# Top-32 attention and two expert layers on one core: score products of a pair of tiles back to back and first, one score copy per pair

## The chip, the cores and the metric

One core of one Trainium2 chip. The time is device microseconds for the whole program, from launch to the last output; three runs of the kernel before stand below, and their median is the time to compare with. All stretches are given in microseconds from the start of the profiled span.

## What is computed

Three layers in sequence. Attention: 4 batches, 8 heads, 576 tokens, head width 64; in every row only the 32 largest scores stay. Then a two-matrix layer with a squared ReLU on 2304 tokens, then a layer in which each token goes to one of eight experts.

```python
scores = scale * np.matmul(q, k.transpose(0, 1, 3, 2))
kth = np.partition(scores, -top_k, axis=-1)[..., -top_k:-top_k + 1]
scores = np.where(scores >= kth, scores, -1000000000.0)
attn = np.exp(scores - np.max(scores, axis=-1, keepdims=True))
attn = attn / (np.sum(attn, axis=-1, keepdims=True) + 1e-09)
x = np.matmul(attn, v)
...
r = np.maximum(x @ w_in, 0.0)
x = (r * r) @ w_out
...
e_idx = np.argmax(xc @ w_gate, axis=1)
y[mask] = gate_w[mask, None] * (np.maximum(xc[mask] @ w1[e], 0.0) @ w2[e])
```

## The kernel before

**Tiles and pairs.** The attention works on 144 tiles of 128 query rows by 576 keys, two at a time: 72 pairs, one pair per turn of the main loop (line 667). fp32 operands are split into a high and a low fp16 part, so a score tile is 2 products for each of three groups of 192 keys, 6 in all, and 12 for a tile that joins the 64 left-over rows of two heads.

**A pair's way through the engines.** PE makes the scores of both tiles in one PSUM tile `pS` (`qk`, line 326). There is one such buffer. ACT copies each tile's scores to SBUF as `s` (`evac_s`, line 334), two copies per pair. DVE builds from `pS` and `s` the arrays of larger and smaller halves `tr` (`tree`, line 351), and only when it has read `pS` may the next pair's scores be written. Then DVE finds the 32 largest values by four rounds of MAX8 (line 370) and three of MATCH_REPLACE8 (line 373). ACT derives the exponent's bias `nm` from the first round (line 378) and takes the exponentials (line 392); DVE makes the mask `mk` (line 397); POOL applies it (line 405); ACT rounds to fp16 and sums (line 420), POOL forms the low part (line 425), a DMA transposes, and three pairs later PE multiplies with V (`av`, line 448) and ACT scales the result (line 466). ACT also keeps three of each tile's 32 values for a later test: `keep_bounds`, line 401, once per pair.

**The tree of the next pair stands at the end of a pair's turn on DVE.** `tree(a + 2)` is put behind `top32(a)` and the two masks of the pair come behind it, so DVE needs the next pair's second score copy as soon as the current pair's fourth round is done.

**The first expert-like layer runs between the pairs.** From the tenth pair on, PE also does the products of the two-matrix layer for tokens that are finished: `mm1` (line 525, into `ph`), on ACT three passes (lines 533, 535, 537), on POOL one (line 546), and `mm2` (line 558, into `px`). A turn of the loop issues about 4.4 half units of it, in two parts; between them stand the scores of the next pair's second tile:

```python
        if nxt:
            qk(a + 2)
            evac_s(a + 2)
        conv(conv_act, j, 0, 2)
        step_units(HALVES / 2)
        if nxt:
            qk(b + 2)
            evac_s(b + 2)
        step_units(HALVES / 2)
```

What is left of that layer when the last pair is done runs after the attention; then come the routing and the experts.

**What sets the order.** The code's order is only the start: a scheduler with a model of the engines arranges the instructions of every engine when the program is built, and each engine then executes its own list strictly in order. The wait of one instruction holds everything behind it on that engine.

Of the kernel before, what the change touches and what calls it, by code (L numbers as in the profile page):

```python
# [9 lines left out]
F32 = mybir.dt.float32  # L10
# [5 lines left out]
AF = mybir.ActivationFunctionType  # L16
# [5 lines left out]
B, H, S, D = 4, 8, 576, 64  # L22
# [16 lines left out]
SB = 3  # L39
# [60 lines left out]
def attention_two_moes(ctx, tc, qm, qc, kd, vd, w_in, w_out, w_g, w1, w2, cst, out):  # L100
    nc = tc.nc
# [7 lines left out]
    apool = att_scope.enter_context(tc.tile_pool(name="att", bufs=1, side="right"))  # L109
# [18 lines left out]
    bounds = const.tile([128, B * H * S // 128, 3], F32, name="bounds")  # L128
# [177 lines left out]
    st = [dict() for _ in range(NTILE)]  # L306

    def kv(kind, vi, hd):
        return vq[kind, visits[vi]["b"], visits[vi]["pr"], hd]

    def qk(i):
        vi, tl = T[i]
        if i % 2 == 0:
            st[i]["ps2"] = st[i + 1]["ps2"] = side[0].tile([128, 2, 3, 256], F32, name="pS")
        ps = st[i]["ps"] = st[i]["ps2"][:, i % 2, :, :192]
        if tl[0] == "m":
            c0 = tl[1] * 128 if visits[vi]["half"] else tl[1] * 256 + tl[2] * 128
            jobs = [(vq[vi, "qm"][:, :, c0:c0 + 128], kv("k", vi, tl[1]))]
        else:
            q = vq[vi, "qc"]  # L320
            jobs = [(q[:, :, 0:128], kv("k", vi, 0)), (q[:, :, 64:192], kv("k", vi, 1))]
        for c in range(3):
            n = 0
            for q, kh in jobs:
                for part in range(2):
                    nc.tensor.matmul(ps[:, c], lhsT=q[:, part], rhs=kh[:, c * 192:(c + 1) * 192],  # L326
                                     start=(n == 0), stop=(n == 2 * len(jobs) - 1))
                    n += 1

    def evac_s(i):  # L330
        if i % 2 == 0:
            st[i]["s2"] = st[i + 1]["s2"] = apool.tile([128, 2, S], F32, name="s", bufs=SB)
        s = st[i]["s2"][:, i % 2]
        nc.scalar.activation(s.rearrange("p (a b) -> p a b", a=3), st[i]["ps"], AF.Copy,  # L334
                             scale=2.0 ** (-2 * QK_EXP))
        st[i]["s"] = s

    def pair_tiles(a):
        m = apool.tile([128, 2, 32], F32, name="m8", bufs=3)
        nm = apool.tile([128, 2], F32, name="nm", bufs=3)  # L340
        l = apool.tile([128, 2, 2], F32, name="l", bufs=6)
        for k in range(2):
            st[a + k].update(m=m[:, k], nm=nm[:, k:k + 1], l=l[:, :, k])
        st[a]["pair"] = (m, nm, l)

    def tree(a):
        R2 = apool.tile([128, 2, S], F32, name="tr")
# [50 lines left out]
        st[i]["mk"] = t  # L398

    def keep_bounds(a):  # L400
        nc.scalar.activation(bounds[:, a:a + 2], st[a]["pair"][0][:, :, 15::8], AF.Copy)

    def apply_mask(i):
        e = st[i]["e"]
# [223 lines left out]
    def fetch(j):  # L628
        for pc in by_rj.get(j, []):
            if "raw" not in pc:  # L630
                load_piece(pc)
# [11 lines left out]
    def conv(step, j, lo, hi):  # L643
        for it in conv_at.get(j, [])[lo:hi]:
            step(*it)
# [6 lines left out]
    conv(load_w64, -1, 0, 4)  # L652
    nc.sync.dma_start(wgs, w_g)
    qk(0)
    evac_s(0)
    qk(1)
    conv(conv_act, -1, 0, 2)
    conv(conv_dve, -1, 0, 2)
    conv(conv_split, -1, 0, 2)
    conv(conv_act, -1, 2, 4)  # L660
    conv(conv_dve, -1, 2, 4)
    evac_s(1)
    fetch(-1)
    conv(load_w64, 0, 0, 2)
    run_all(low_pool)

    for j in range(NJ + AV_LAG + 1):
        a, b = 2 * j, 2 * j + 1
        live = a < NTILE
        nxt = a + 2 < NTILE  # L670
# [6 lines left out]
        conv(conv_split, j - 1, 2, 4)  # L677
        conv(load_w64, j, 2, 4)
        if nxt:
            qk(a + 2)  # L680
            evac_s(a + 2)
        conv(conv_act, j, 0, 2)
        step_units(HALVES / 2)
        if nxt:
            qk(b + 2)
            evac_s(b + 2)
        step_units(HALVES / 2)
        conv(conv_dve, j, 0, 2)
        if live:
# [123 lines left out]
    pair = side[0].tile([128, 2, 512], F32, name="pS")  # L813
# [592 lines left out]
```

## Time and profile before

| | |
|---|---|
| median of three runs | 1046.55 us (1044.35, 1046.55, 1052.29) |
| the profiled execution, its own time | 1045.87 us |
| its span on the core | 1044.0 us |
| busy: DVE, PE, ACT, POOL | 845.9, 792.5, 772.9, 764.2 us (81, 76, 74, 73% of the span) |
| mean granted TensorE clock | 0.926 |

The program has three stretches that matter here. Until about 193 us the weights are converted beside the first twelve pairs. From 193 to 767 us the other sixty pairs run, about 9.6 us each, with the two-matrix layer between them. From 767 us the rest of that layer, the routing and the experts follow. The shares of the whole span mix these stretches, so every reading below is of one stretch. In the rows, "idle before" is the time in which an engine stood still ahead of an instruction, with what ended it; "PE" rows are products, and PEclk is the granted clock as a share of 2.4 GHz.

### The profile page before, as it was taken

To read this page: it belongs to the slowest core of one execution; us is meant where nothing else is said; L and a number is where in the kernel's file an instruction comes from. 1 tells how busy PE (TensorE), PEld (TensorE's weight loads), DVE (VectorE), ACT (ScalarE), POOL (GpSimd) and SP (SyncE) were. 2 spreads that over 40 slices of the span, in tenths; PEclk is the share of its full clock that TensorE was granted. 3 is DMA by queue.
4 is the path that set the end of the run, shared out by engine and by line. 5 is a ranking of instruction groups with operands and counts; after the bars stand their busy time and mean duration, and the time that the engine had idled before them with its cause. 6 is when DMAs were issued, how large, how long until landed. Compare 5 with 4: busy or idle time off the path is not lost. (4 is left out here: it accounts for less than half of the span.)

```text
span 1044.0 us, 25879 instructions
## 1 busy us (share of the span) xinstructions
PE 792.5 (76%) x9036; PEld 603.1 (58%) x9036; DVE 845.9 (81%) x2279; ACT 772.9 (74%) x2237; POOL 764.2 (73%) x783
## 2 busy tenths in 40 slices
PE   0213238989799879979879997979998876888863
PEld 0113137767577667667557775757776654565632
DVE  3999999989999999998997878899965927543641
ACT  6777777999889888887787887879987643443720
POOL 4675777898879888887788877788984686462860
PEclk9999999999889979989869998969999897998986
DMA  8765454567575474565575466454547616671600
GB/s 278 192 164 160 112 135 80 112 129 144 122 142 121 98 135 103 100 138 95 123 122 101 106 113 132 103 122 80 107 88 241 220 52 232 245 240 57 220 17 15
DMA packets 257024, 138.16 MB, mean 132 GB/s; under 512 B 215348, under 2 KB 238260, under 8 KB 256848
## 3 DMA queue, kind: packets, MB, share of 16 engines
q1 hardware_dynamic: 253568, 132.16, 54.0%
q0 software_dynamic: 3280, 3.80, 1.1%
q8 instruction: 93, 1.52, 0.6%
q14 instruction: 83, 0.68, 0.2%
HBM read 76.92 MB, written 7.37 MB: 81 GB/s over the span
## 5 line engine op out<-in xcount | busy, mean ns | idle before, releaser
L370 DVE MAX8 m<-tr 128x8 f32<-128x288 f32 (+1 forms) x576 | 276.8, 518 | 0.0
L405 POOL TENSOR_TENSOR e<-e,mk 128x576 f32<-128x576 f32 x144 | 196.1, 1374 | 25.7 <-DVE mk L397 25.7
L425 POOL TENSOR_TENSOR phl<-e,phl 128x576 f16<-128x576 f32 x144 | 187.3, 1309 | 14.7 <-ACT phl L420 13.0
L558 PE MATMUL px<-woh,gh 128*128 128x512 f16 x576 | 190.5, 381 | 10.0 <-POOL gh L546 6.5
L373 DVE MATCH_REPLACE8 tr<-m,tr 128x288 f32<-128x288 f32 x432 | 187.2, 439 | 0.0
L448 PE MATMUL misc<-vh,pt 128*128 128x64 f16 (+1 forms) x2400 | 124.2, 203 | 66.0 <-ACT xn L466 34.3
L525 PEld LDWEIGHTS <-wih 128*128 128x128 f16 x2048 | 145.0, 101 | 46.9 <-issue 13.3
L546 POOL TENSOR_TENSOR gh<-g,gh 128x128 f16<-128x128 f32 (+1 forms) x256 | 124.6, 492 | 64.8 <-ACT gh L537 47.0
L525 PE MATMUL ph<-xb,wih 128*128 128x128 f16 (+1 forms) x1792 | 159.9, 232 | 12.2 <-DMA xb<-xhl 10.0
L448 PEld LDWEIGHTS <-pt 128*128 128x128 f16 (+1 forms) x2400 | 104.9, 103 | 86.6 <-issue 57.2
L351 DVE SCALAR_TENSOR_TENSOR tr<-pS,s 128x576 f32<-128x576 f32 x144 | 102.2, 751 | 53.6 <-ACT s L334 51.3
L558 PEld LDWEIGHTS <-gh 128*128 128x128 f16 x864 | 77.5, 100 | 70.3 <-POOL gh L546 14.6
L326 PE MATMUL pS<-kh,ql 128*128 128x192 f16 x576 | 76.4, 279 | 48.5 <-DMA kh<-lp 18.2
L392 ACT ACTIVATE e<-s,nm 128x576 f32<-128x576 f32 x144 | 111.1, 773 | 1.4 <-POOL phl L425 0.8
L558 PE MATMUL px<-wol,gh 128*128 128x512 f16 x288 | 109.4, 380 | 0.0
L334 ACT ACTIVATE s<-pS 128x576 f32<-128x576 f32 x144 | 92.5, 642 | 18.3 <-PE pS L326 18.0
L420 ACT ACTIVATE phl<-e 128x577 f16<-128x577 f32 x144 | 98.2, 682 | 4.3 <-POOL e L405 3.8
L525 PE MATMUL ph<-xb,wil 128*128 128x128 f16 (+1 forms) x896 | 97.2, 231 | 0.0
L533 ACT ACTIVATE r<-ph 128x128 f32<-128x128 f32 (+1 forms) x256 | 72.0, 289 | 30.3 <-PE ph L525 28.3
L326 PEld LDWEIGHTS <-ql 128*128 128x128 f16 x576 | 56.9, 111 | 63.8 <-issue 43.0
L535 ACT ACTIVATE g<-r 128x128 f32<-128x128 f32 (+1 forms) x256 | 83.3, 327 | 8.7 <-POOL gh L546 5.1
L397 DVE TENSOR_SCALAR mk<-s,m 128x576 f16<-128x576 f32 x144 | 85.0, 631 | 0.0
(229 smaller groups left out, 1644.1 us busy)
## 6 DMA issues: line engine op xcount, KB each, us to landing
wraw<-in_w SPq DMA_DIRECT2D x64, 512.0 KB
wol<-in_w_in SPq DMA_DIRECT2D x16, 512.0 KB
raw<-in_qm SPq DMA_DIRECT2D x48, 128.0 KB
w<-in_w_out SPq DMA_DIRECT2D x10, 512.0 KB
raw<-in_vd SPq DMA_DIRECT2D x32, 160.0 KB
raw<-in_kd SPq DMA_DIRECT2D x16, 288.0 KB
out<-x SPq DMA_DIRECT2D x16, 256.0 KB
wol<-in_w_out SPq DMA_DIRECT2D x6, 512.0 KB
```

Source lines behind the costliest of these rows:

```text
L326: nc.tensor.matmul(ps[:, c], lhsT=q[:, part], rhs=kh[:, c * 192:(c + 1) * 192], start=(n == 0), stop=(n == 2 * len(jobs) - 1))
L351: last = nc.vector.scalar_tensor_tensor(out=R2[:, :, n * 288:n * 288 + 288].rearrange("p k (c x) -> p k c x", c=3), in0=near, scalar=2.0 * ...
L370: return both(lambda k: nc.vector.max(m[k][:, 8 * r:8 * r + 8], x[k][:, :n]))
L373: both(lambda k: nc.vector.match_replace(out=dst[k][:, :n], in_to_replace=m[k][:, 8 * r:8 * r + 8], in_values=src[k][:, :n], imm_value=NEG))
L392: nc.scalar.activation(e[:, :S], st[i]["s"], AF.Exp, scale=0.125, bias=st[i]["nm"])
L405: nc.gpsimd.tensor_mul(e[:, :S], e[:, :S], st[i]["mk"])
L420: nc.scalar.activation(h[:, 0, :S + 1], st[i]["e"], AF.Copy, accum_out=st[i]["l"][:, 0:1])
L425: nc.gpsimd.tensor_sub(h[:, 1, :S], st[i]["e"][:, :S], h[:, 0, :S])
L448: nc.tensor.matmul(ps[:, a, :], lhsT=pt[:rows, 5 * low + c, :], rhs=vh[:rows, c, part * D:(part + 1) * D], start=(n == 0), stop=(n == len( ...
L525: nc.tensor.matmul(ph, lhsT=wt[:, d, u["f"] * 128:(u["f"] + 1) * 128], rhs=x[:, :, c0 + d, :], start=(n == 0), stop=(n == 11))
L546: g_last[0] = nc.gpsimd.tensor_sub(u["gh"][:, 1], u["g"], u["gh"][:, 0]).ins
L558: nc.tensor.matmul(px, lhsT=gh[:, part, t * 128:(t + 1) * 128], rhs=w[:, f, :], start=(f == 0 and n == 0), stop=(f == 15 and n == 2))
```

## The change

Four edits. In the loop one call, `scores(a + 2)`, takes the place of the two separate steps: it issues the products of both tiles and one copy, under `tc.high_priority()`, which makes the scheduler take them ahead of other ready work. `evac_s` copies both tiles with one ACT instruction. The tile `m8` holds three pairs, and `keep_bounds` copies for three pairs at once. Before the loop, the first pair's copy stands behind the first weight conversions. In the changed kernel the lines behind these functions have numbers 9 or 10 higher, and behind the loop 5 higher.

```diff
-    def evac_s(i):
-        if i % 2 == 0:
-            st[i]["s2"] = st[i + 1]["s2"] = apool.tile([128, 2, S], F32, name="s", bufs=SB)
-        s = st[i]["s2"][:, i % 2]
-        nc.scalar.activation(s.rearrange("p (a b) -> p a b", a=3), st[i]["ps"], AF.Copy,
+    def evac_s(a):
+        s2 = apool.tile([128, 2, S], F32, name="s", bufs=SB)
+        nc.scalar.activation(s2.rearrange("p k (c x) -> p k c x", c=3), st[a]["ps2"][:, :, :, :192], AF.Copy,
                              scale=2.0 ** (-2 * QK_EXP))
-        st[i]["s"] = s
+        for k in range(2):
+            st[a + k].update(s2=s2, s=s2[:, k])
+
+    def scores(a):
+        with tc.high_priority():
+            qk(a)
+            qk(a + 1)
+            evac_s(a)
+
+    m6 = [None]
 
     def pair_tiles(a):
-        m = apool.tile([128, 2, 32], F32, name="m8", bufs=3)
+        if a % 6 == 0:
+            m6[:] = [m6[-1], apool.tile([128, 6, 32], F32, name="m8", bufs=3)]
+        m = m6[-1][:, a % 6:a % 6 + 2]
...
-        st[a]["pair"] = (m, nm, l)
+        st[a].update(pair=(m, nm, l), six=m6[-1])
...
     def keep_bounds(a):
-        nc.scalar.activation(bounds[:, a:a + 2], st[a]["pair"][0][:, :, 15::8], AF.Copy)
+        if a % 6 == 4:
+            nc.scalar.activation(bounds[:, a - 4:a + 2], st[a]["six"][:, :, 15::8], AF.Copy)
...
     qk(0)
-    evac_s(0)
     qk(1)
...
-    evac_s(1)
+    evac_s(0)
...
         if nxt:
-            qk(a + 2)
-            evac_s(a + 2)
+            scores(a + 2)
         conv(conv_act, j, 0, 2)
         step_units(HALVES / 2)
-        if nxt:
-            qk(b + 2)
-            evac_s(b + 2)
         step_units(HALVES / 2)
```

PE of the kernel before, the 46th pair (scores in `pS_7885`): here the six products of the first tile end, and products of probabilities with V follow.

```order
L326 LDWEIGHTS ql_7722
L326 MATMUL pS_7885<-kh_6476,ql_7722 128x192
L448 LDWEIGHTS pt_7680
L448 MATMUL misc_8024<-vh_7720,pt_7680 128x64
L448 LDWEIGHTS pt_7680
L448 MATMUL misc_8024<-vh_7720,pt_7680 128x64
```

And this is where the second tile of that pair begins, behind the products of the two-matrix layer's second half (`px`).

```order
L558 LDWEIGHTS gh_8708
L558 MATMUL px_7785<-woh_89,gh_8708 128x512
L558 LDWEIGHTS gh_8708
L558 MATMUL px_7785<-wol_87,gh_8708 128x512
L326 LDWEIGHTS ql_7722
L326 MATMUL pS_7885<-kh_6477,ql_7722 128x192
```

Between the two places stand 54 other products. PE of the changed kernel, the same pair (`pS_7782`), at the step from the first tile (keys `kh_6391`) to the second (`kh_6392`):

```order
L326 LDWEIGHTS ql_7622
L326 MATMUL pS_7782<-kh_6391,ql_7622 128x192
L326 LDWEIGHTS ql_7622
L326 MATMUL pS_7782<-kh_6391,ql_7622 128x192
L326 LDWEIGHTS ql_7622
L326 MATMUL pS_7782<-kh_6392,ql_7622 128x192
L326 LDWEIGHTS ql_7622
L326 MATMUL pS_7782<-kh_6392,ql_7622 128x192
```

Nothing stands between the two tiles any more. ACT of the kernel before, the 43rd pair: the second row behind its first copy is the first row here, and its second copy (`s_7492<-pS_7485`) is the last.

```order
L533 ACTIVATE r_7964<-ph_7919 128x256
L466 ACTIVATE xn_7306<-misc_7549,l_7016 128x64
L466 ACTIVATE xn_7308<-misc_7549,l_7016 128x64
L535 ACTIVATE g_7966<-r_7964 128x256
L537 ACTIVATE gh_7968<-r_7964 128x256
L533 ACTIVATE r_8084<-ph_7951 128x256
L392 ACTIVATE e2_94<-s_7328,nm_7508 128x576
L242 ACTIVATE vh_7720<-raw_7537 128x5x64
L535 ACTIVATE g_8086<-r_8084 128x256
L537 ACTIVATE gh_8088<-r_8084 128x256
L401 ACTIVATE bounds_85<-m8_7507 128x6
L334 ACTIVATE s_7492<-pS_7485 128x576
```

ACT of the changed kernel, the same pair: the bias of the pair before it (`nm_7410`) and the one copy of both tiles (`s_7402<-pS_7389`).

```order
L387 ACTIVATE nm_7410<-m8_7124 128x2
L430 ACTIVATE phl2_100,l_7297<-e2_94 128x577
L221 ACTIVATE raw_7338<-raw_7338 128x256
L332 ACTIVATE s_7402<-pS_7389 128x1152
L430 ACTIVATE phl0_98,l_7297<-e0_92 128x577
L401 ACTIVATE e1_93<-s_7241,nm_7410 128x576
L476 ACTIVATE xn_7213<-misc_7450,l_6925 128x64
L476 ACTIVATE xn_7215<-misc_7450,l_6925 128x64
L543 ACTIVATE r_7835<-ph_7797 128x256
L401 ACTIVATE e2_94<-s_7241,nm_7410 128x576
L543 ACTIVATE r_7860<-ph_7822 128x256
L411 ACTIVATE bounds_85<-m8_7124 128x18
```

The copy has moved from the end of the pair's ACT work to its beginning. Over the 14th to the 72nd pair the copy that completes a pair's scores stands 11 instructions behind the bias of the pair before it in the middle case, and 13 ahead of its own pair's bias; in the changed kernel 3 behind and 21 ahead. On DVE the order of the instructions of these pairs is the same in both kernels.

## Rows read from the trace of the kernel before

**Rows 1.** Busy time by stretch: start:end, length, engines, PEclk, DMA share, GB/s

```profile
core 0: us, PE busy (x) PEld busy (x) DVE busy (x) ACT busy (x) POOL busy (x), PEclk, DMA share, GB/s
193.00:767.00 574.00, 511.75 (x6053) 394.25 (x6050) 526.47 (x1527) 494.63 (x1573) 472.58 (x523) 0.92 0.59 115
536.00:637.00 101.00, 96.69 (x1075) 73.07 (x1076) 78.48 (x232) 85.09 (x257) 78.27 (x86) 0.98 0.58 110
767.00:858.00 91.00, 80.12 (x868) 59.34 (x866) 52.44 (x168) 58.67 (x190) 63.07 (x83) 0.96 0.52 164
858.00:1044.00 186.00, 127.89 (x1354) 93.54 (x1353) 90.88 (x168) 75.56 (x120) 97.77 (x63) 0.84 0.42 144
```

**Rows 2.** Waits from 193 to 767 us: total us, times, longest

```profile
DVE tr L351 <- ACT s L334: 43.6, 27, 4.3
...
ACT s L334 <- PE pS L326: 14.7, 10, 3.6
...
PE pS L326 <- ACT s L334: 9.4, 11, 1.4
...
PE pS L326 <- DVE tr L351: 3.5, 3, 1.9
```

**Rows 3.** Timeline around the 46th pair: start us, us, instruction, idle before

```profile
501.44 1.04 PE L525 MATMUL ph<-xb,wih 128*128 128x256 f16 x8
502.31 0.66 PE L326 MATMUL pS<-kh,ql 128*128 128x192 f16 x6
502.81 1.35 PE L448 MATMUL misc<-vh,pt 128*128 128x64 f16 x30
504.09 0.61 PE L525 MATMUL ph<-xb,wil 128*128 128x256 f16 x4
...
508.20 0.59 PE L558 MATMUL px<-woh,gh 128*128 128x512 f16 x2
508.63 0.38 PE L558 MATMUL px<-wol,gh 128*128 128x512 f16 x1
508.85 0.66 PE L326 MATMUL pS<-kh,ql 128*128 128x192 f16 x6
...
510.23 1.42 DVE L351 SCALAR_TENSOR_TENSOR tr<-pS,s 128x576 f32<-128x576 f32 x2 [1.56 <-ACT s L334]
```

**Rows 4.** Timeline around the 43rd pair

```profile
475.51 0.66 PE L326 MATMUL pS<-kh,qm 128*128 128x192 f16 x6
...
479.20 0.22 ACT L401 ACTIVATE bounds<-m 128x6 f32<-128x6 f32 x1
479.31 0.66 ACT L334 ACTIVATE s<-pS 128x576 f32<-128x576 f32 x1
...
480.00 1.42 DVE L351 SCALAR_TENSOR_TENSOR tr<-pS,s 128x576 f32<-128x576 f32 x2 [3.40 <-ACT s L334]
```

**Rows 5.** Groups by line, 193 to 767 us: busy us, mean ns, idle before

```profile
L351 DVE SCALAR_TENSOR_TENSOR tr<-pS,s 128x576 f32<-128x576 f32 x118 | 83.8, 751 | 45.7 <-ACT s L334 43.6
...
L334 ACT ACTIVATE s<-pS 128x576 f32<-128x576 f32 x118 | 75.9, 644 | 14.8 <-PE pS L326 14.7
...
L401 ACT ACTIVATE bounds<-m 128x6 f32<-128x6 f32 x59 | 13.0, 220 | 0.4
```

**Rows 6.** Groups by line, whole span: an ACT copy of 1024 elements

```profile
L870 ACT ACTIVATE w10h<-wraw 128x1024 f16<-128x1024 f32 x12 | 12.2, 1048 | 6.2 <-PEq L1131 4.1 <-DMA wraw<-in_w 2.0
```

**Rows 7.** Busy time, 767 to 858 us, of line 525 alone, then of line 558 alone

```profile
767.00:858.00 91.00, 37.03 (x516) 33.60 (x516) 0.96 0.52 164
...
767.00:858.00 91.00, 38.18 (x140) 12.59 (x138) 0.96 0.52 164
```

**Rows 8.** Busy time by 4 us, columns as in rows 1

```profile
444.00:448.00 4.00, 0.69 (x6) 0.69 (x7) 4.00 (x15) 4.00 (x12) 3.27 (x3) 1.00 0.39 107
448.00:452.00 4.00, 2.09 (x23) 1.85 (x22) 4.00 (x8) 1.68 (x6) 3.15 (x3) 0.54 1.07 221
452.00:456.00 4.00, 4.00 (x38) 3.07 (x37) 4.00 (x17) 3.86 (x10) 4.00 (x4) 0.61 0.54 106
```

## Prediction, made before the changed kernel ran

> **What bounds the kernel now.** I read the busy times by stretch first, then the waits of the pairs' stretch, then the timeline at two pairs where DVE waited, and last the stretch behind the attention.
>
> In the stretch of the last sixty pairs, 193 to 767 us, DVE is busy for 526.5 of 574.0 us, PE for 511.8, ACT for 494.6 and POOL for 472.6 [rows 1]. All four are loaded, but DVE most, and it has almost one reason to stand still: 43.6 of its 47.5 idle us are 27 waits of the tree for a score copy [rows 2]. That is what the change goes for. From one tree to the next there are 59 steps, so a pair takes 574.0 / 59 = 9.73 us now, and 526.5 / 59 = 8.92 us if DVE never waited.
>
> Why is the copy late? Two pairs show two causes. At the 46th, PE makes the first tile's scores at 502.31 us and the second's only at 508.85 us: 54 other products stand between them in its list. The tree starts at 510.23 us, after 1.56 us of idling [rows 3]. At the 43rd, PE is done at 475.51 + 0.66 = 476.17 us, but ACT copies the second tile only at 479.31 us, behind the other instructions that its list has ahead of it, the last of them the copy of the bounds; DVE idles 3.40 us [rows 4]. So the second tile is late once on PE and once on ACT, and in both cases by its place in a list, not by its own length.
>
> PE is the second bound, locally: between 536 and 637 us it is busy 96.7 of 101 us at a clock of 0.98, while DVE is busy for 78.5 [rows 1]. Behind the attention, from 767 to 858 us, PE is busy 80.1 of 91 us with the rest of the two-matrix layer; the 186 us from there to the end wait for that layer, as the routing needs its output.
>
> **The change part by part.**
>
> *The order of scores and copy.* The lists show that it does what it says: the second tile's products follow the first's at once, and the copy stands near the head of the pair's ACT work. What is late next? From the end of one tree to the start of the next DVE needs 8.92 less the tree's two instructions of 0.751 us [rows 5], so 7.4 us. Within this come PE's 12 products at 0.083 us (six take 502.31 to 502.81 us, and the last ends 0.16 us later [rows 3]), 1.16 us, and the one copy. It isn't in the trace. 1024 elements take 1.048 us [rows 6] and 576 take 0.644 us [rows 5], 0.90 ns for each element more, so 1152 take 0.644 + 576 x 0.00090 = 1.16 us. A hand-over adds 0.03 us (the copy's end at 479.97 to the tree's start at 480.00 us [rows 4]). That is 2.4 us, and about 5.0 us are left by which PE and ACT together may come late before DVE notices. Before, the 54 products in between took most of this away: 5.9 us at the 46th pair.
>
> PE comes late when its list holds more than a DVE period of work between two pairs' scores. I weigh the products in both lists with the pitch in [rows 3]: 0.109 us for 256 columns (eight in 0.87 us) and half of it for 128, 0.215 us for 512, 0.083 us for 192, 0.043 us for 64 (thirty in 1.28 us). From the 13th to the 71st pair both lists hold the same sum, 463 and 461 us, or 7.8 us a pair. But it is spread otherwise: the fullest pair has 12.0 us before and 9.9 us now, the emptiest 1.5 and 4.4 us, and the eight pairs from the 50th to the 57th, which fill the stretch around 536 to 637 us, hold 82.1 before and 66.8 us now. There PE's 96.7 us should shrink by 66.8 / 82.1 to 78.7 us, the same as DVE's 78.5. So I expect most of DVE's idling there to go (101 - 78.5 = 22.5 us), with some 4 us left because the two engines are then level. Of the other 43.6 - 22.5 = 21.1 us I leave 4 us too, for the pairs in which the clock is at its lower level. Saved: 43.6 - 8 = 35.6 us. The ends are 0 (PE or ACT then makes DVE wait as long as before) and 43.6 us.
>
> *One copy for two.* 2 x 0.644 - 1.16 = 0.13 us of ACT's time a pair, 8 us over 59. *Bounds once per three pairs.* 59 copies of 0.220 us [rows 5] become 20, 8.6 us of ACT's time less, at most 0.2 us back for their greater length. Neither is on DVE's path; ACT idles 574.0 - 494.6 = 79.4 us in this stretch, so I take both at 0 on the end. Their ends: 16.6 us gained if ACT is what comes late each time, and a loss, since the one copy waits for all 12 products: 0.5 us longer than for six, at the head of ACT's list, where the exponentials and the passes of the two-matrix layer queue behind it. ACT waits 14.7 us for scores now [rows 2]; 59 x 0.5 = 30 us more would still fit into its idle time. In return PE no longer waits for the first tile's copy before it writes the second: 9.4 us [rows 2].
>
> *What is pushed behind the attention.* The same lists show a price. From the last pair's first score product on, PE's list holds 648 products of line 525 instead of 564, and 166 of line 558 instead of 150. By pitch the 84 and 16 more cost 84 x 0.055 + 16 x 0.215 = 8.0 us; by their share of the busy time there (37.03 / 516 and 38.18 / 140 us [rows 7]) 10.4 us. Lower end 0: PE idles 91 - 80.1 = 10.9 us there and could fill it. I take 8.0 us. Most of what is issued less for it (5.9 us) stands between the tenth and the 13th pair, where DVE's weight conversions set the pace, and gives nothing back there.
>
> *The sum.* 1045.87 - 35.6 + 8.0 = 1018.3 us against the profiled execution; the median of the runs is 0.7 us above it, so 1019 us.
>
> **The rivals.**
>
> *The wait changes its owner.* PE at 511.8, ACT at 494.6 and POOL at 472.6 us would have to fit into 574.0 - 35.6 = 538 us, so shares of 95, 92 and 88%, in lists that hold each other up. If the dense pairs keep their 22.5 us, because PE is as full in practice as now, and of the other 21.1 us a third stays, 14 us are saved, and with 8.0 us behind the attention the time is 1040.5 us. For it: PE's 96.7 of 101 us. Against it: the lists' sums there, and that DVE's idling sits in pairs whose second tile was late by its place.
>
> *Everything goes.* All 43.6 us, and the added products vanish in the 10.9 us of PE's idle time: 1003 us. For it: 5.0 us of room. Against it: PE and DVE are level in the dense pairs.
>
> *Slower, by PE's wait at the head of its list.* The scores stand first, and the one buffer `pS` is free only after the tree. Wherever PE is early it now waits there with the whole two-matrix layer behind it, where before it waited 3.5 us for the tree in all [rows 2]. Standing still costs it more than the wait: from 444 to 448 us it is busy for 0.69 of 4 us, and from 448 to 456 us the granted clock is 0.54 and 0.61, so a large part of the time at 1.2 instead of 2.4 GHz [rows 8]. The mean of 0.92 over the stretch [rows 1] means 0.08 x 574 = 46 us of PE's time lost. PE's own bound is 511.8 us busy and its 62.2 us of idling less the 12.9 us at the scores, 561 us. The kernel gets slower when that passes 574 - 8 = 566 us, so from 5 us more of lost clock or new waits on. With half as much lost again, 23 us, the stretch takes 584 us, and the time is 1046.5 + 10 + 8 = 1064.5 us. Against it: pairs with less than 5 us of PE work are 10 in the list before and 3 in the new one, and these are the ones in which PE ran dry.
>
> The Trainium skill speaks for this rival ("TensorE: Matmul & The Clock Gate", section "HAM oscillation — how this bites in real kernels"): gaps in PE's work bring the clock down to half, and the work behind the gap pays. The trace agrees with it at 444 to 456 us. By that rule alone many waits for the tree would make PE the bound, as in the rival; but a smoother list would also raise the clock, which would help the forecast.
>
> **How the numbers follow.** Forecast, 1019 us: 0.56, with a range of its own from 1008 us (all 43.6 us saved, 5 us pushed back) to 1031 us (23.5 us saved, 8 us pushed back). The wait changes its owner, around 1040 us: 0.20. Everything goes, 1003 us: 0.12. Slower by PE's wait, from 1050 us up with 1064 us in the middle: 0.12. A measurement of this kernel tells about 1% from no change, 10.5 us. Faster by more: the forecast, everything goes, and a third of the second case (below 1036 us), 0.74. Within 1%: the rest of the second case and a little of the last, 0.15. Slower: 0.11. For 8 in 10 the range leaves out part of each end: 1004 to 1044 us.
>
> **What would show it.** Right: the tree's wait for the score copy falls from 43.6 to about 8 us, the pairs' stretch takes about 538 us, the two-matrix layer behind it takes some 8 us longer than 91 us, and the mean clock of the stretch isn't below 0.92. Wrong: if the tree's wait falls and DVE or POOL waits elsewhere for as long, the second case holds; if PE waits at line 326 for the tree for tens of us and the clock falls, the last; if the stretch behind the attention grows by much more than 8 us, I have mis-sized what was pushed there.

## The result and the profile after

| | kernel before | changed kernel |
|---|---|---|
| median, runs on the same chip | 1048.29 us (4 runs, 1044.35 to 1052.29) | 1023.65 us (4 runs, 1023.59 to 1025.36) |
| ratio, 95% interval | | 0.976 (0.973 to 0.979) |
| the profiled execution, its own time | 1045.87 us | 1023.65 us |
| its span | 1044.0 us | 1021.8 us |
| mean granted clock | 0.926 | 0.946 |

The kernel became 24.6 us faster by the medians and 22.2 us by the two profiled executions; 27.5 us were forecast. The direction, the place and the range held. Of the runs of the experiments below, one of e4's four, 1213.85 us at a granted clock of 0.688, fell into a slow state of the chip and stands in none of its numbers. The page of the changed kernel, its busy times over the whole span:

```profile
PE 779.8 (76%) x9036; PEld 592.5 (58%) x9036; DVE 845.7 (83%) x2279; ACT 759.8 (74%) x2117; POOL 767.4 (75%) x783
```

The stretches are cut at the same events in both kernels: the 13th pair's tree, the last tree, and the end of the last PE transpose of the two-matrix layer's output. First the changed kernel, by windows; the second row is a piece of the first, from the 50th pair's tree to the 58th's.

```profile
core 0: us, PE busy (x) PEld busy (x) DVE busy (x) ACT busy (x) POOL busy (x), PEclk, DMA share, GB/s
191.50:730.20 538.70, 492.63 (x6009) 376.26 (x6005) 529.63 (x1527) 479.51 (x1464) 470.07 (x517) 0.97 0.64 122
532.60:604.90 72.30, 71.75 (x802) 54.92 (x801) 71.21 (x205) 66.18 (x182) 65.89 (x67) 1.00 0.62 129
730.20:830.40 100.20, 88.65 (x974) 65.57 (x973) 53.60 (x168) 64.58 (x214) 69.14 (x90) 0.96 0.50 149
830.40:1021.80 191.40, 131.46 (x1358) 97.49 (x1358) 88.19 (x168) 76.20 (x121) 98.02 (x64) 0.81 0.41 141
```

And the kernel before, cut in the same way (its 13th pair's tree starts at 193.1 us, and the long stretch from there is in [rows 1]).

```profile
546.70:636.10 89.40, 85.56 (x971) 64.42 (x969) 69.11 (x205) 75.96 (x231) 69.62 (x77) 1.00 0.54 109
767.20:856.60 89.40, 79.21 (x861) 58.57 (x859) 52.44 (x168) 57.87 (x189) 61.78 (x81) 0.96 0.52 163
856.60:1044.00 187.40, 128.60 (x1359) 94.23 (x1358) 90.88 (x168) 76.16 (x121) 98.86 (x64) 0.84 0.42 144
```

So the 22.2 us are: 1.6 us less before the 13th pair (191.5 for 193.1), 35.4 us less between the two trees (574.1 to 538.7), 10.8 us more behind the last tree, and 4.0 us more from there to the end. Of the 35.4 us, 17.1 come from eight pairs alone, the 50th to the 57th: 89.4 us before, 72.3 now. DVE is busy there for the same 69 to 71 us in both kernels; it now works nearly without a pause (1.1 us of idle time for 20.3).

The waits of the changed kernel from 191.5 to 730.2 us, against [rows 2]:

```profile
DVE tr L360 <- ACT s L332: 5.1, 3, 3.4
...
ACT s L332 <- PE pS L326: 3.0, 5, 1.5
...
PEld L326 <- DVE tr L360: 2.4, 6, 0.8
...
PE pS L326 <- DVE tr L360: 0.5, 2, 0.3
```

The tree waits for a score copy three times for 5.1 us, where it waited 27 times for 43.6 us. ACT's own wait for scores falls from 14.7 to 3.0 us, and PE's wait for the first tile's copy, 9.4 us before, is not in the list any more. The 46th pair, which [rows 3] show of the kernel before, by the timeline:

```profile
486.40 1.15 PE L326 MATMUL pS<-kh,ql 128*128 128x192 f16 x12
...
489.94 0.47 ACT L242 ACTIVATE vh<-raw 128x320 f16<-128x320 f32 x1 [3.63 <-DMA raw<-in_vd]
...
492.68 1.12 ACT L332 ACTIVATE s<-pS 128x1152 f32<-128x1152 f32 x1
...
493.83 1.42 DVE L360 SCALAR_TENSOR_TENSOR tr<-pS,s 128x576 f32<-128x576 f32 x2 [1.26 <-ACT s L332]
```

All twelve products stand in one block and the copy is one instruction. This pair is also one of the three that still wait, and for a new reason: ACT's list stood still for 3.63 us at a late load of V, and the score copy was behind it. The largest of the three waits, 3.36 us, is at the 50th pair, where PE was held up at the products of the two-matrix layer by a transfer, and makes the scores only behind them.

```profile
525.21 1.89 PE L535 MATMUL ph<-xb,wih 128*128 128x256 f16 x8 [2.82 <-DMA xb<-xhl]
...
531.44 1.13 ACT L332 ACTIVATE s<-pS 128x1152 f32<-128x1152 f32 x1
...
532.60 1.42 DVE L360 SCALAR_TENSOR_TENSOR tr<-pS,s 128x576 f32<-128x576 f32 x2 [3.36 <-ACT s L332]
```

The groups by line, 191.5 to 730.2 us (busy us, mean ns, idle before), against [rows 5]:

```profile
L360 DVE SCALAR_TENSOR_TENSOR tr<-pS,s 128x576 f32<-128x576 f32 x119 | 84.5, 750 | 9.2 <-ACT s L332 5.1
...
L406 DVE TENSOR_SCALAR mk<-s,m 128x576 f16<-128x576 f32 x118 | 75.6, 680 | 0.0
...
L332 ACT ACTIVATE s<-pS 128x1152 f32<-128x1152 f32 x59 | 65.9, 1116 | 3.1 <-PE pS L326 3.0
...
L411 ACT ACTIVATE bounds<-m 128x18 f32<-128x18 f32 x20 | 4.7, 237 | 0.0
```

The one copy takes 1.116 us (1.16 were estimated), two small ones took 1.288. The bounds fall from 13.0 to 4.7 us of ACT's time. DVE's mask grew from 627 ns before to 680 ns; the last section comes back to it. In the kernel before, by the same view from 193 to 767 us:

```profile
L397 DVE TENSOR_SCALAR mk<-s,m 128x576 f16<-128x576 f32 x118 | 69.3, 627 | 0.0
```

### The profile page after: what moved, and what is told of

It is laid out like the page before. It is cut to its first block, busy times and chain, and to the rows that moved or that the text cites. A ratio compares the mean times of both kernels' runs of the same rounds, so it can differ in the third digit from the quotient of the medians.

```text
span 1021.8 us, 25759 instructions
## 1 busy us (share of the span) xinstructions
PE 779.8 (76%) x9036; PEld 592.5 (58%) x9036; DVE 845.7 (83%) x2279; ACT 759.8 (74%) x2117; POOL 767.4 (75%) x783
## 3 DMA queue, kind: packets, MB, share of 16 engines
q8 instruction: 94, 1.54, 0.6%
## 5 line engine op out<-in xcount | busy, mean ns | idle before, releaser
L435 POOL TENSOR_TENSOR phl<-e,phl 128x576 f16<-128x576 f32 x144 | 190.6, 1328 | 33.2 <-ACT phl L430 29.0
L568 PE MATMUL px<-woh,gh 128*128 128x512 f16 x576 | 189.3, 382 | 15.9 <-POOL gh L556 10.8
L535 PE MATMUL ph<-xb,wih 128*128 128x128 f16 (+1 forms) x1792 | 156.6, 231 | 21.0 <-DMA xb<-xhl 9.5
L458 PE MATMUL misc<-vh,pt 128*128 128x64 f16 (+1 forms) x2400 | 119.3, 198 | 63.7 <-ACT xn L476 33.7
L556 POOL TENSOR_TENSOR gh<-g,gh 128x128 f16<-128x128 f32 (+1 forms) x256 | 130.2, 515 | 41.1 <-ACT gh L547 27.4
L458 PEld LDWEIGHTS <-pt 128*128 128x128 f16 (+1 forms) x2400 | 100.8, 100 | 85.3 <-issue 53.2
L360 DVE SCALAR_TENSOR_TENSOR tr<-pS,s 128x576 f32<-128x576 f32 x144 | 102.1, 750 | 14.8 <-ACT s L332 10.8
L326 PE MATMUL pS<-kh,ql 128*128 128x192 f16 x576 | 67.2, 273 | 38.9 <-DMA kh<-lp 26.1
L406 DVE TENSOR_SCALAR mk<-s,m 128x576 f16<-128x576 f32 x144 | 93.3, 688 | 0.0
L332 ACT ACTIVATE s<-pS 128x1152 f32<-128x1152 f32 x72 | 80.3, 1116 | 3.7 <-PE pS L326 3.4
L547 ACT ACTIVATE gh<-r 128x128 f16<-128x128 f32 (+1 forms) x256 | 80.7, 320 | 1.3 <-PE px L568 1.0
```

What stands on the lines that cost most here:

```text
L360: last = nc.vector.scalar_tensor_tensor(out=R2[:, :, n * 288:n * 288 + 288].rearrange("p k (c x) -> p k c x", c=3), in0=near, scalar=2.0 * ...
L406: nc.vector.tensor_scalar(out=t, in0=st[i]["s"], scalar1=st[i]["m"][:, 31:32], scalar2=None, op0=ALU.is_ge)
L435: nc.gpsimd.tensor_sub(h[:, 1, :S], st[i]["e"][:, :S], h[:, 0, :S])
L458: nc.tensor.matmul(ps[:, a, :], lhsT=pt[:rows, 5 * low + c, :], rhs=vh[:rows, c, part * D:(part + 1) * D], start=(n == 0), stop=(n == len( ...
L535: nc.tensor.matmul(ph, lhsT=wt[:, d, u["f"] * 128:(u["f"] + 1) * 128], rhs=x[:, :, c0 + d, :], start=(n == 0), stop=(n == 11))
L556: g_last[0] = nc.gpsimd.tensor_sub(u["gh"][:, 1], u["g"], u["gh"][:, 0]).ins
```

## The experiments

The theory: the second tile's scores were late by their place in a list, and what put them there is one of the change's edits. The rivals for it are the order in the code with its priority, the number of copies, the copy that stood between the two tiles, and the bounds on ACT. "Tree waits" is the total of the row "DVE tr <- ACT s"; "stretch" runs from the 13th to the last tree; "layer behind" runs from there to the last transpose; all three are in us, of the profiled execution. "Apart" counts, of the 59 pairs from the 14th on, those in which PE does other products between the last score product of the first tile and the first one of the second; I counted them in the traces. Ratios are to runs of the kernel before on the same chip.

| kernel | median us | ratio (95%) | tree waits | stretch | layer behind | apart |
|---|---|---|---|---|---|---|
| before | 1048.29 | 1 | 43.6 | 574.1 | 89.4 | 51 |
| changed | 1023.65 | 0.976 (0.973 to 0.979) | 5.1 | 538.7 | 100.2 | 0 |
| e1: bounds alone | 1039.43 | 0.990 (0.987 to 0.993) | 42.5 | 572.6 | 90.9 | 53 |
| e2: no priority | 1022.26 | 0.975 (0.970 to 0.981) | 3.5 | 540.6 | 99.1 | 0 |
| e5: two copies behind both tiles | 1024.9 | 0.976 (0.971 to 0.981) | 2.9 | 538.7 | 99.0 | 0 |
| e8: a copy between the tiles | 1042.88 | 0.993 (0.990 to 0.996) | 42.0 | 574.2 | 89.3 | 54 |
| e4: bounds per pair | 1025.38 | 0.977 (0.972 to 0.983) | 4.4 | 538.0 | 99.6 | 0 |
| e7: coded apart, one copy | 1019.77 | 0.971 (0.966 to 0.976) | 3.5 | 536.3 | 98.9 | 2 |
| e9: one copy and nothing else | 1022.91 | 0.975 (0.972 to 0.978) | 2.5 | 537.7 | 98.6 | 3 |

The first four kernels behind "changed" ran beside one another (before: 1048.92 us), so did e4, e7 and the first two variants (1049.68), and so did e9 and the third (1050.61).

**e1, the bounds alone.** The kernel before with the bounds of three pairs copied at once.

```diff
+        if a % 6 == 0:
+            m6[:] = [m6[-1], apool.tile([128, 6, 32], F32, name="m8", bufs=3)]
+        m = m6[-1][:, a % 6:a % 6 + 2]
...
-        nc.scalar.activation(bounds[:, a:a + 2], st[a]["pair"][0][:, :, 15::8], AF.Copy)
+        if a % 6 == 4:
+            nc.scalar.activation(bounds[:, a - 4:a + 2], st[a]["six"][:, :, 15::8], AF.Copy)
```

> The kernel before with one part of the change: bounds kept once per three pairs (24 copies for 72). The place theory (the gain comes from the second tile's products and copy no longer standing late in PE's and ACT's lists) expects no gain: a ratio to the kernel before of 0.995 to 1.005, and still some 35 to 45 us of waits of the tree for the score copy in the pairs' stretch. The load theory (the gain is ACT's saved time, half of it from the bounds) expects about half of the gain, a ratio near 0.988.

Its stretch by windows and its waits:

```profile
191.20:763.80 572.60, 508.17 (x6027) 390.72 (x6026) 526.86 (x1527) 489.35 (x1528) 470.89 (x520) 0.93 0.59 115
...
DVE tr L355 <- ACT s L334: 42.5, 25, 3.8
```

The trees wait as before. Yet the median of ten runs (1035.51 to 1043.84 us) is 9.5 us below the kernel before, while the profiled execution, at 1043.48 us the second longest of the ten, shows a span only 2.3 us shorter. Where the other runs gained is not in this profile and stays open. The ratio of 0.990 is a miss for the place theory, which expected 0.995 to 1.005, and lies near the 0.988 of the load theory; what speaks against the load theory is that the trees wait as long as before and that, taken out of the changed kernel, the bounds are worth nothing that can be told (e4, below).

**e2, no priority.**

```diff
     def scores(a):
-        with tc.high_priority():
-            qk(a)
-            qk(a + 1)
-            evac_s(a)
+        qk(a)
+        qk(a + 1)
+        evac_s(a)
```

> The changed kernel without the high priority: both tiles' products and then the one copy stand together in the code, as ordinary work. If the scheduler's priority makes the gain, the ratio to the kernel before goes back towards 1 (0.99 or above) and the tree waits 20 us or more. The place theory expects the full gain, a ratio of 0.973 to 0.980, since the products still stand back to back in PE's list, and tree waits below 10 us.

Tree waits 3.5 us, stretch 540.6 us, ratio 0.975: all of the gain without the priority. With the constants as they are here, it isn't the priority.

**e5, two copies, both behind the second tile.**

```diff
-        nc.scalar.activation(s2.rearrange("p k (c x) -> p k c x", c=3), st[a]["ps2"][:, :, :, :192], AF.Copy,
-                             scale=2.0 ** (-2 * QK_EXP))
         for k in range(2):
+            nc.scalar.activation(s2[:, k].rearrange("p (c x) -> p c x", c=3), st[a + k]["ps"], AF.Copy,
+                                 scale=2.0 ** (-2 * QK_EXP))
```

> The changed kernel with two score copies, both behind the products of both tiles. ACT gets back about 0.13 us a pair, 8 us over the stretch. The load theory expects 4 us or more of the gain lost (ratio to the kernel before 0.980 to 0.985). The place theory expects the full gain, 0.973 to 0.980, and tree waits below 10 us.

```profile
193.00:731.70 538.70, 493.70 (x5995) 378.17 (x5993) 530.44 (x1527) 483.03 (x1522) 470.68 (x516) 0.97 0.64 122
...
DVE tr L360 <- ACT s L333: 2.9, 1, 2.9
```

ACT is busy for 483.0 us instead of 479.5 in the stretch, the trees wait 2.9 us, the ratio is the same, 0.976. The number of copies is worth nothing; ACT's 3.5 us lie in its idle time.

**e8, together and with priority, but a copy between.** `evac_s` is again that of the kernel before, with one copy for each tile, also before the loop.

```diff
     def scores(a):
         with tc.high_priority():
             qk(a)
+            evac_s(a)
             qk(a + 1)
-            evac_s(a)
+            evac_s(a + 1)
```

> The changed kernel with two copies, the first between the products of the two tiles, all four steps together in the code and with the high priority; bounds still once per three pairs. The second tile's first product then waits for ACT, as both tiles share a PSUM bank. The place theory, sharpened (the copy in between is what drives the two tiles' products apart), expects the gain to be gone: ratio 0.993 to 1.005, tree waits of 30 us or more, products of the second tile 2 to 5 us behind the first's. If coding the steps together or the priority made the gain, the ratio stays at 0.973 to 0.985.

The stretch and the waits, and the pair whose tree starts at 567.11 us by the timeline:

```profile
190.50:764.70 574.20, 513.88 (x6077) 395.33 (x6075) 529.67 (x1526) 493.23 (x1538) 471.33 (x523) 0.93 0.60 115
...
DVE tr L362 <- ACT s L334: 42.0, 25, 4.2
...
PE pS L326 <- ACT s L334: 11.0, 11, 2.6
...
559.53 0.66 PE L326 MATMUL pS<-kh,ql 128*128 128x192 f16 x6
...
561.15 0.63 ACT L334 ACTIVATE s<-pS 128x576 f32<-128x576 f32 x1
...
564.03 1.15 PE L326 MATMUL pS<-kh,qc 128*128 128x192 f16 x12
...
567.11 0.76 DVE L362 SCALAR_TENSOR_TENSOR tr<-pS,s 128x576 f32<-128x576 f32 x1 [3.67 <-ACT s L334]
```

The stretch is back at 574.2 us and the tree waits at 42.0 us, with the products together in the code and first in priority. PE again waits for the first tile's copy before it writes the second tile, 11.0 us, as in [rows 2], and in 54 of 59 pairs other products stand between the two tiles; here the second tile comes 3.84 us behind the end of the first (559.53 + 0.66 to 564.03 us). That the scheduler plans for PE's wait and fills the place is my reading of these lists; its reasons are not on record. The expectation put the wait down to a PSUM bank that the two tiles share. No run tested the bank, so which part of sharing the one buffer `pS` causes it stays open. The median is 6.0 us below the kernel before although the stretch is as long, and the ratio of 0.993 lies just at the edge of the expected 0.993 to 1.005; as in e1, the bounds of three pairs are in this kernel too, and the profile of one execution doesn't show where that comes from.

**e4, the bounds once per pair again.** `pair_tiles` and `keep_bounds` as in the kernel before, the rest as in the changed kernel.

```diff
-        if a % 6 == 4:
-            nc.scalar.activation(bounds[:, a - 4:a + 2], st[a]["six"][:, :, 15::8], AF.Copy)
+        nc.scalar.activation(bounds[:, a:a + 2], st[a]["pair"][0][:, :, 15::8], AF.Copy)
```

> The changed kernel with the bounds kept once per pair again. Keeping them once per three pairs gave 0.990 on the kernel before, though its pairs' stretch was hardly shorter there. If that part adds to the rest, this run loses it: ratio to the kernel before 0.984 to 0.988. The place theory expects nothing lost in the stretch (536 to 542 us, tree waits below 10 us) and a ratio of 0.973 to 0.980.

0.977 against 0.976: no difference. ACT has room for the bounds once the order is right.

**e7, coded apart, with one copy.** The two tiles stand where they stood in the loop of the kernel before, without priority, and one copy follows the second.

```diff
         if nxt:
-            scores(a + 2)
+            qk(a + 2)
         conv(conv_act, j, 0, 2)
         step_units(HALVES / 2)
+        if nxt:
+            qk(b + 2)
+            evac_s(a + 2)
         step_units(HALVES / 2)
```

> The changed kernel with the two tiles' products at the two old places of the code, half of the two-matrix layer's work between them, no priority, and one copy behind the second. In PE's list the two tiles stand back to back all the same in most pairs. If it is the copy in between that drove them apart, this has the whole gain: ratio 0.973 to 0.980, stretch 536 to 543 us, tree waits below 10 us. If the place in the code makes the gain, the ratio is 0.985 or above.

The whole gain is there, with tree waits of 3.5 us and a ratio of 0.971, if anything a little better. Half units of the two-matrix layer stand between the two tiles in the code, but in PE's list the tiles follow each other in 57 of 59 pairs once no copy lies between them.

**e9, one copy and nothing else.** e7 still had the bounds of the change. This is the kernel before with one edit, `evac_s` as in the change and called once, behind the second tile (before the loop too):

```diff
         if nxt:
             qk(a + 2)
-            evac_s(a + 2)
...
         if nxt:
             qk(b + 2)
-            evac_s(b + 2)
+            evac_s(a + 2)
```

> The kernel before with nothing changed but the score copy: one for both tiles, at the old place of the second one. Bounds once per pair, no priority, the two tiles' products at their two old places in the code. If the removed copy between the products is the whole cause, this alone has the gain: ratio to the kernel before 0.971 to 0.980, stretch 535 to 543 us, tree waits below 10 us. If the change needs its other parts too, the ratio is 0.985 or above.

```profile
190.90:728.60 537.70, 493.57 (x6006) 378.95 (x6004) 530.83 (x1527) 485.08 (x1504) 469.62 (x517) 0.97 0.66 122
...
DVE tr L350 <- ACT s L332: 2.5, 4, 1.0
...
561.47 1.16 PE L326 MATMUL pS<-kh,qc 128*128 128x192 f16 x12
...
564.39 1.13 ACT L332 ACTIVATE s<-pS 128x1152 f32<-128x1152 f32 x1
...
565.62 1.42 DVE L350 SCALAR_TENSOR_TENSOR tr<-pS,s 128x576 f32<-128x576 f32 x2
```

The window, the waits, and one pair of the dense part (the twelve products stand in one block). The whole gain comes with this edit: no copy between two products into one buffer. e9 also makes one copy of two, but e5 and e8 both have two copies, issued together and with priority, and differ in the place of the first copy alone: 538.7 us with it behind both tiles, 574.2 us with it between them. So it is the place of the first copy and not the number or the length of the copies.

**The price behind the attention.** The second question was the 10.8 us behind the last tree. If they are the pushed products, a kernel that pulls them forward should get part of it back. `AV_LAG` is the number of pairs by which the product with V trails, `X_LAG` the turns that finished tokens wait before the two-matrix layer may take them, `HALVES` the half units per turn.

```diff
-AV_LAG = 3
+AV_LAG = 2
```

> The changed kernel with the product of probabilities and V two pairs behind instead of three, so that tokens are ready earlier and less of the two-matrix layer is left behind the attention: 600 products of its first and 159 of its second half from the last pair's scores on, for 648 and 166. By the pitch of the trace that is 48 x 0.0556 + 7 x 0.215 = 4.2 us. If PE's work there sets the end, the time is about 1019.5 us (ratio to the kernel before near 0.972) with the stretch unchanged; if the transposes come too late for the earlier products, PE waits for them and the stretch is longer, ratio 0.977 or above.

```diff
-AV_LAG = 3
+AV_LAG = 2
-HALVES = 4.4
+HALVES = 5.2
-X_LAG = 2
+X_LAG = 1
```

> As the run before, and also with tokens released to the two-matrix layer one pair earlier and 5.2 instead of 4.4 half units a turn: 569 and 153 products are left. 79 x 0.0556 + 13 x 0.215 = 7.2 us less than in the changed kernel. If PE's work behind the attention sets the end, about 1016.5 us, ratio near 0.970. If the fuller pairs (10.8 us of PE work at most, for 9.9) make the tree wait again, the stretch grows by 5 us or more and the ratio is 0.975 or above.

The third takes the same three constants with the loop of e7.

> One copy for both tiles and bounds once per three pairs, the products at the two old places, no priority; and the two-matrix layer pulled ahead: V products two pairs behind, tokens released one pair earlier, 5.2 half units a turn. From the last pair's scores on PE's list holds 528 and 142 products of that layer, for 648 and 166 in the changed kernel: 120 x 0.0556 + 24 x 0.215 = 11.8 us less. If PE's work behind the attention sets the end and DVE keeps its pace, about 1012 us and a ratio of 0.960 to 0.967, with the time from the last tree to the end of that layer near 100 - 12 = 88 us. If the fullest pair of PE work (13.6 us) makes the tree wait again, the stretch is 543 us or longer and the ratio 0.970 or above.

| kernel | median us | ratio (95%) | tree waits | stretch | layer behind | apart |
|---|---|---|---|---|---|---|
| v1: AV_LAG 2 | 1023.8 | 0.976 (0.971 to 0.980) | 1.7 | 544.2 | 94.1 | 1 |
| v2: all three constants | 1017.11 | 0.970 (0.965 to 0.974) | 0.9 | 537.3 | 95.3 | 1 |
| v3: the three in the loop of e7 | 1031.67 | 0.983 (0.980 to 0.986) | 16.5 | 554.7 | 92.3 | 11 |

All three shorten the layer behind the attention, by 4.9 to 7.9 us. Two of them lose time in the stretch. The products with V now come a pair earlier, and PE waits for the transposed probabilities `pt`, for which it doesn't wait in this stretch of the changed kernel. First v1, then v3:

```profile
PEld L458 <- DMA pt<-phl: 20.5, 27, 1.9
...
PE misc L458 <- DMA pt<-phl: 13.2, 20, 1.7
```

```profile
191.50:746.20 554.70, 504.83 (x6105) 387.88 (x6102) 534.27 (x1528) 486.49 (x1483) 472.91 (x523) 0.96 0.60 118
...
PEld L452 <- DMA pt<-phl: 25.1, 18, 5.7
...
PE misc L452 <- DMA pt<-phl: 17.8, 13, 5.6
...
DVE tr L354 <- ACT s L332: 16.5, 11, 3.3
```

In v3 the trees wait 16.5 us again; v3 is a miss. In v1 the trees hardly wait, but DVE is busy for 538.2 us instead of 529.6: 4.9 of these 8.6 us are in line 245, which makes the low part of V (21.6 us for 16.7; 19.3 in the changed kernel's second profile), and 2.8 in the mask (78.4 us for 75.6). Both end a fixed time behind an instruction of POOL under which they start (last section), so they grow with POOL's work beside them; the wait for `pt` is not shown to be what v1 pays. v2 has the same wait for `pt`, at 8.0 us, without losing by it.

v2 and v3 have the same constants and differ only in the loop: in v2 `scores(a + 2)` stands as one call with priority, in v3 the two tiles are coded apart without it. The tree's wait of v2 in the stretch:

```profile
DVE tr L360 <- ACT s L332: 0.9, 1, 0.9
```

The trees of v3 wait 16.5 us, and the stretch takes 537.3 us in v2 and 554.7 in v3. With the old constants the same difference in the loop was worth nothing (e7 against the changed kernel). So the order in the code and the priority do count once the work between the pairs is pulled ahead; which of the two, no run shows.

**v2 and the changed kernel beside each other**, both once more, five runs each; the kernel before has 1047.12 us there.

> The changed kernel once more, beside the next run on the same chip: ratio to the kernel before 0.973 to 0.979, stretch 536 to 542 us, about 100 us from the last tree to the end of the two-matrix layer.

> The variant with V products two pairs behind, tokens released one pair earlier and 5.2 half units a turn, timed beside the changed kernel on the same chip. If the work pushed behind the attention has a price, it is faster than the changed kernel by 4 to 7 us (the first time 6.5 us by the medians, on different chips), and from the last tree to the end of the two-matrix layer it takes about 95 us for about 100. If the first difference was one between chips, the two agree within 2 us.

The changed kernel gives 1023.79 us, 0.976 (0.974 to 0.979), and v2 1015.25 us, 0.969 (0.967 to 0.972): v2 is 8.5 us faster than the change and beats both kernels. Its windows by the same cuts:

```profile
192.50:731.30 538.80, 496.15 (x6047) 380.60 (x6048) 531.13 (x1529) 481.12 (x1468) 471.66 (x518) 0.97 0.63 122
731.30:825.30 94.00, 82.31 (x871) 60.11 (x867) 53.55 (x168) 60.12 (x194) 66.05 (x84) 0.95 0.52 159
```

The stretch is the changed kernel's (538.8 and 538.7 us), PE has 88.65 - 82.31 = 6.3 us less to do behind the last tree, and that part is 6.2 us shorter. So what stands behind the attention costs nearly its full time.

## Why the prediction was right, step by step

**The tree's waits**, forecast to go from 43.6 to 8 us, went to 5.1. The reading of [rows 3 and 4] held: late by place, not by length. The working took the two edits to the order together, the call with its priority and the one copy; e5, e8 and e9 show that only the copy's leaving the middle counts, and that with these constants the order of the code and the priority do nothing. The sum did not suffer by that, since it was made from the lists of the whole change. I had read the 54 products between the tiles as a matter of their order; they go with the copy in between, and so with the wait of [rows 2], "PE pS <- ACT s", which I listed as a small side gain of 9.4 us. The 4 us that I left for pairs at the lower clock are not what remained: 1.26 and 3.36 of the 5.1 us stand behind two late transfers, of V and of `xb`. And that the stretch took 538.7 us where 538 were forecast is in part luck: 2.9 us more of the waits went, and DVE's own work grew by 3.1 us.

**The dense pairs.** From the lists' sums I expected PE and DVE to become level in the eight pairs from the 50th on, at 78.7 and 78.5 us of work for what had taken 101 us. PE's busy time there went from 85.6 to 71.75 us, a factor of 0.84 where the lists gave 66.8 / 82.1 = 0.81, and DVE has 71.2 us: level, in 72.3 us. This is 17.1 us of the gain, where 22.5 - 4 = 18.5 were forecast. Two errors met in that: the 101 us of the forecast begin with the 49th pair, and the eight pairs alone took 89.4 us with 20.3 us of DVE's idling; and of the 4 us that were to be left only 1.1 are, while DVE's work there grew by 2.1. Weighing two lists by pitch told rightly that PE would make room.

**One copy and the bounds**, taken as 0: e5 and e4 agree, each within the interval of the changed kernel. The 9.5 us of e1 on the kernel before are not explained by it.

**What is pushed behind the attention**: 8.0 us by pitch, measured 10.8 between equal cuts. Behind the last tree the trace counts 600 products of line 535 (525 before), 84 more, as in the lists, and 162 of line 568 (558 before). Their busy time, in the window from 730.2 to 830.4 us, first 535 and then 568:

```profile
730.20:830.40 100.20, 41.90 (x600) 38.17 (x600) 0.96 0.50 149
...
730.20:830.40 100.20, 43.62 (x162) 15.13 (x162) 0.96 0.50 149
```

Against [rows 7] that is 4.9 + 5.4 = 10.3 us more. The term was mis-sized mostly in the second line: 16 x 0.215 = 3.4 us were counted, and 5.4 came. The lists were counted from the last pair's first score product, and from there the traces have the same 150 and 166 products. But the time is taken from the last tree, which comes some 5 to 7 us later, and by then the kernel before had done 10 of them and the changed one 4, so that 22 more were left. With 22, the pitch gives 84 x 0.055 + 22 x 0.215 = 9.4 us, and the share of the busy time, which stood in the prediction as the upper bound of 10.4 us, gives 12.0; the measured 10.8 us lie between them. The lower end, that PE's 10.9 us of idle time would take it in, was wrong: by the equal cuts PE's busy time grew by 88.65 - 79.21 = 9.4 us, and its idle time did not shrink but went from 10.2 to 11.6 us.

**What the sum left out.** With 35.4 us for 35.6 in the stretch, the 5.4 us between the forecast 27.6 and the measured 22.2 (profiled executions) are 2.8 us behind the last tree, 4.0 us at the end and 1.6 us the other way before the 13th pair. DVE is busy 529.6 instead of 526.5 us in the stretch; its mask alone takes 75.6 - 69.3 = 6.3 us more, and other lines give half of that back. And the 4.0 us from the last transpose to the end were not foreseen. Part of them could be one wait for a weight load of the experts, by the waits of the changed kernel behind 730 us,

```profile
PE ph L1042 <- DMA wraw<-in_w: 5.4, 1, 5.4
```

but e9 doesn't have this wait and its last part is still 193.2 us long. What makes the end longer in the kernels with the short stretch (190 to 195 us, and 187.4 before) is not settled. The granted clock is 0.81 there, 0.84 before.

**The rivals.** "The wait changes its owner" did not come true: the dense pairs gave up 17.1 of 89.4 us, though PE is busy there for 71.75 of 72.3 us. "Everything goes" was near for the waits (5.1 us left) and wrong about the end. "Slower, by PE's wait at the head of its list" needed tens of us at line 326; there are 2.4 + 0.5 us. And the clock went the other way, from 0.92 to 0.97 in the stretch. The piece that stood in [rows 8] begins 3.9 us behind the 39th pair's tree; PE was busy there for 0.69 + 2.09 + 4.00 us, at a clock of 1.00, 0.54 and 0.61. In the changed kernel that tree starts at 426.9 us, and the same piece behind it is

```profile
430.80:434.80 4.00, 3.79 (x42) 2.57 (x40) 4.00 (x16) 3.99 (x12) 3.29 (x5) 1.00 0.02 6
434.80:438.80 4.00, 3.80 (x46) 3.08 (x43) 4.00 (x7) 4.00 (x15) 2.48 (x3) 1.00 0.95 172
438.80:442.80 4.00, 2.46 (x44) 1.96 (x44) 4.00 (x16) 4.00 (x14) 3.92 (x4) 1.00 0.50 123
```

At 1.00 - 0.97 the clock takes some 16 us of PE's time in the stretch, where it took 46, and PE's busy time fell from 511.8 to 492.6 us. The Trainium skill ("TensorE: Matmul & The Clock Gate", section "HAM oscillation — how this bites in real kernels") says that gaps in PE's work are paid for at half clock by the work behind them. The trace agrees, in the direction that helped: PE stands still for 46.1 us of the stretch instead of 62.2, and the clock is 0.97 instead of 0.92.

## What to carry to other kernels

When a scheduler makes the lists, look for a reader that stands between two writers of the same buffer. Here a row of 9.4 us of waits was its mark; with it, other products stood between the two writers in 51 of 59 pairs, for 2.5 us in the middle case, and the stretch was 35 us longer. Move the reader behind both writers before touching priorities or the order of the code: that one edit gave everything here. The other two come next, when more work is pulled between the pairs: then the same loop without them lost 17 us of the stretch (v3 against v2). Where work is pushed to a place with nothing beside it, expect it to cost nearly its full time, count it from the cut at which the time is taken, and then see whether its inputs can be ready earlier (v2: 8.5 us).

## What the runs showed of the hardware

**A mask on DVE that starts under an instruction of POOL ends 0.32 us behind it.** The same mask instruction takes from 0.51 us up to three times that. In the changed kernel, behind the 59th pair's tree, by the timeline, and then the durations of the two masks of this pair (ns, least, median, longest):

```profile
614.56 1.28 POOL L435 TENSOR_TENSOR phl<-e,phl 128x576 f16<-128x576 f32 x1 [0.50 <-PE ph L535]
614.91 1.68 DVE L406 TENSOR_SCALAR mk<-s,m 128x576 f16<-128x576 f32 x2
616.47 0.43 POOL L556 TENSOR_TENSOR gh<-g,gh 128x128 f16<-128x128 f32 x1 [0.63 <-ACT gh L547]
...
L406 DVE TENSOR_SCALAR mk<-s,m x2: 508/877/1246, 614.9 to 616.1; 128x576 f16<-128x576 f32 x2
```

The first mask starts while POOL is at its low part and takes 1.246 us, ending 0.32 us after POOL's 615.84; the second has POOL idle beside it but for its last 0.1 us and takes 0.508 us. The same holds over the whole stretch, by my count in the traces. Of 117 masks that start between 193 and 730.2 us in the changed kernel, 67 start when an instruction of POOL has 0.2 us or more to go; every one of them ends 0.31 or 0.32 us behind that instruction, after 0.53 to 1.54 us in all, and the other 50 take 0.53 us in the mean (one of them 1.50, which starts 0.03 us ahead of an instruction of POOL and ends 0.31 us behind it). In the kernel before, from 193 to 767 us, it is 38 masks of 118, also with 0.31 or 0.32 us. The instructions of line 245 do the same, 0.35 us behind POOL, in 14 of 24 cases in the changed kernel and 17 of 24 in v1. So the mask's mean of 680 ns instead of 627 goes with more masks that start beside POOL's work. The Trainium skill ("SBUF — State Buffer", section "Who interferes with whom") says that DVE, in its two-port modes, which a `tensor_scalar` like the mask can enter, and POOL share a pair of ports, that whichever issues first has it for its whole instruction, and that the other stands still meanwhile. The trace agrees: the mask's end hangs on POOL's end and not on its own start, and 0.19 of its own 0.51 us pass while POOL still works. No run here took POOL's work away to test it.

**The copy from PSUM.** 576 elements more cost 1.116 - 0.644 = 0.472 us, 0.82 ns each, less than the 0.90 ns worked out from [rows 5 and 6].
